# A fused attention and GLU block on one core: the orders of all five engines searched anew

## The chip, the cores and the metric

The kernel runs on one core of a Trainium2 chip. The metric is the device time of one execution in microseconds (us). A profile's span is about 2 us shorter than the device time of the same run, so spans are compared with spans only.

## The reference

All data are bfloat16: 2048 tokens (16 tiles of 128), width 448, hidden width 1792.

```python
def _A_ref(x, wqkv, wo):                 # linear attention, 16 heads of 28
    q, k, v = split_heads(x @ wqkv)
    phi = lambda t: where(t > 0, t + 1, exp(t)) + 1e-6
    pq, pk = phi(q), phi(k)
    kv = einsum("bhsd,bhse->bhde", pk, v)
    den = einsum("bhqd,bhd->bhq", pq, pk.sum(tokens)) + 1e-6
    return (einsum("bhqd,bhde->bhqe", pq, kv) / den) @ wo
def _B_ref(x, w_gate, w_up, w_down):
    return (gelu(x @ w_gate) * (x @ w_up)) @ w_down
h  = x + _A_ref(layernorm(x), wqkv, wo)
h2 = h + _B_ref(layernorm(h), w_gate, w_up, w_down)
```

The keys need all tokens before any query can be finished, so the program has a joint: everything up to `kv`, then the queries, the second layernorm, gate/up and down.

## The kernel before

Every piece of work is a task with a number. A task knows what it reads and writes; from that the program derives its semaphore waits. Which task an engine issues next is not derived: it is read from five strings of numbers, one for each of TensorE (PE), ACT, VectorE (DVE), GpSimd (POOL) and the sync engine (SP), which issues the transfers.

```python
ORDERS = (
    "26 34 32 43 41 63 66 71 76 50 ...",   # pe
    "3 25 29 30 38 39 33 42 65 47 ...",    # act
    "27 28 36 37 31 40 35 44 45 54 ...",   # dve
    "17 15 13 0 18 14 20 16 1 21 ...",     # pool
    "2 4 5 6 7 8 9 10 11 12 98 ...",       # sp
)
...
    def place(self, orders):
        self.order = {e: [self.all[int(i)] for i in o.split()] for e, o in zip(ENGS, orders)}
...
    def emit(self, ename, eng):          # cut: each task waits for what it depends on
        for t in self.order[ename]:
            ...
            ins = t.fn(eng, W) if t.mw else t.fn(eng)
```

The tasks, by the names they have in the code, sizes left out (`out2_2` is `out_2` here; the gate/up units keep theirs); the last number is the tile, the pair of tiles p, or the unit v:

- Head: `tr0_t`, `tr1_t` (transposes of tiles 0 to 3 on TensorE), `evxA_t`/`evxD_t` (their evictions), `xT_t` (the same transpose as a transfer, tiles 4 on), `k_t`, `q_t` (projections, source line L404), `ek_t`, `eq_t` (exponentials), `rq_t` (relu), `pt_t` (product of keys with the normalised input, L423), `kv`.
- Middle: `w2_g` (kv folded into wo), `dr_t`, `rd_t`, `pn_t` (denominator, reciprocal, normalised query), `tro_t` (its transpose on TensorE for tiles 0 and 1, L504), `oT_p` (as a transfer for the others), `out_t` (output projection, L523), `trh_t` and `hT_t` (the same two ways for the second layernorm), `wrap_t` (a copy that `hT_t` waits for).
- Back: `gu2_v`, `gu4_v` (gate/up units of two or four tiles), `ge_v` (gelu), `hm_v` (product of gelu and up, L625), `dwd` (load of the down weight), `down_t` (L575), `do_t` (store).

A gate/up unit contracts 448 rows as seven pieces of 64, gate in the upper 64 rows of the array and up in the lower 64, side by side:

```python
for k in range(NK):                       # NK = 7
    W(2 * (NK * jj + k))                  # first one: gate bank psG free
    e.matmul(psG[...], wgu_sb[A_, k, ...], hnT[A_, ka_, ...], start=(k == 0), stop=(k == NK - 1))   # L603
    W(2 * (NK * jj + k) + 1)              # first one: up bank psU free
    e.matmul(psU[...], wgu_sb[B_, k, ...], hnT[B_, kb_, ...], start=(k == 0), stop=(k == NK - 1))   # L605
```

There are two gate banks and two up banks, so unit v waits for the products of unit v-2. All other matmuls named here use one group of 112 or 128 rows: going from one kind to the other is a "switch of row mode".

## Time and profile before

| kernel before | median us | range | runs |
|---|---|---|---|
| ahead of the change | 194.24 | 194.19 to 194.25 | 3 |
| beside the changed kernel | 194.25 | 194.16 to 194.46 | 6 |

The profile on which the prediction rests fell in the slow state (clock 0.95). So that traces at one clock could be compared, the kernel before was profiled again, unchanged, as the run `before_again` (device time 194.41 us, span 192.67 us). I cut its span at four events: the start of `kv`, of the first gate/up unit, of unit gu4_14 and of unit gu4_28. Busy time by stretch in `before_again`; columns: stretch, length, then busy us and instruction count of PE, PEld, DVE, ACT, POOL, then clock, DMA share, GB/s:

```profile
0.00:38.23 38.23, 36.67 (x217) 20.98 (x218) 32.16 (x92) 23.86 (x70) 17.96 (x44) 1.00 0.74 179
38.23:50.79 12.56, 12.34 (x93) 7.09 (x91) 12.31 (x34) 12.09 (x32) 3.35 (x3) 1.00 0.79 137
50.79:83.39 32.60, 32.58 (x446) 23.96 (x447) 31.52 (x88) 12.53 (x37) 18.30 (x24) 1.00 0.59 122
83.39:126.10 42.71, 42.71 (x309) 20.07 (x304) 28.73 (x76) 10.69 (x34) 11.33 (x22) 1.00 0.38 70
126.10:192.67 66.57, 64.12 (x519) 35.25 (x518) 26.96 (x67) 18.44 (x56) 0.00 (x0) 1.00 0.07 22
```

Its chain that ended last, the run of work that decided when the program ended, as shares of the span by engine:

```profile
PE 88%; ACT 4%; DVE 4%; DMA 2%; POOL 1%; issue 0%; DVEq 0%; ACTq 0%; POOLq 0%
```

TensorE is busy nearly all of each stretch. In the second, VectorE and ACT are as full as TensorE; in the third, VectorE is. These two are where an order on those engines can produce a wait; in the last nobody but TensorE counts. "Busy" hides the waits of interest: a matmul that is 0.1 or 0.2 us late leaves the engine "busy" in this count. They are found only by taking each start against the start before it.

### The profile page before, as it was taken

The numbers are of one execution on the slowest core, as the hardware profiler recorded it, in microseconds if no ns is written. First come the engines' busy times: TensorE is split into PE (matmuls) and PEld (weight loads), VectorE is DVE, ScalarE is ACT, GpSimd is POOL, SyncE is SP. The second block draws the span as 40 slices with busy tenths as digits, with TensorE's granted clock in tenths as the row PEclk, the third lists the DMA queues.
The fourth block names the chain that finished last, engine by engine and source line by source line (L and its number), as shares of the span: only waits on it lengthen the run. The fifth ranks groups of instructions, "written<-read, shape, count | busy, mean of one in ns | idle before, by whom it ended". The sixth has DMA issues, their size and how long they took to land.

```text
span 197.8 us, 4145 instructions
## 1 busy us (share of the span) xinstructions
PE 193.7 (98%) x1572; PEld 106.9 (54%) x1572; DVE 132.0 (67%) x355; ACT 78.1 (39%) x226; POOL 50.7 (26%) x92
## 2 busy tenths in 40 slices
PE   7999999999999999999999999999999999999995
PEld 7554555555767776654454445444444454444454
DVE  3899988999999989988786537244445422444412
ACT  3797645599943324141330420023444200334200
POOL 7067710640451955235222024000000000000000
PEclk9999999999999999999999999999999999999999
DMA  6966449994587046420217272600200010100011
GB/s 194 375 174 88 94 96 209 221 215 63 102 291 124 16 50 117 102 53 23 56 26 153 57 56 52 133 21 30 46 0 3 0 46 4 46 0 3 0 46 46
DMA packets 35331, 16.97 MB, mean 86 GB/s; under 512 B 27696, under 2 KB 34032, under 8 KB 35312
## 3 DMA queue, kind: packets, MB, share of 16 engines
q1 hardware_dynamic: 35168, 16.60, 38.4%
q8 instruction: 12, 0.20, 0.4%
q10 hardware_dynamic: 144, 0.11, 0.2%
q14 instruction: 7, 0.06, 0.1%
HBM read 8.26 MB, written 1.84 MB: 51 GB/s over the span
## 4 chain that ended last, share of the span: by engine, by line
PE 90%; DMA 4%; DVE 4%; POOL 1%; issue 0%; DVEq 0%; POOLq 0%
PE ps L603 42%; PE ps L575 22%; PE ps L404 9%; PE ps L523 7%; PE ps L423 5%; PE ps L605 3%; DMA x_sb<-in_A_x_dram 2%; DVE st L348 2%; DMA xnT<-xnn 2%; DVE pk L417 1%; PE ps L471 0%; PE ps L462 0%; POOL wqk_sb L302 0%; PE ps L550 0%; DVE xnn L370 0%; DVE mv L349 0%
## 5 line engine op out<-in xcount | busy, mean ns | idle before, releaser
L605 PE MATMUL ps<-hnT,wgu_sb 64*128 64x512 bf16 (+1 forms) x490 | 89.9, 342 | 0.0
L603 PE MATMUL ps<-hnT,wgu_sb 64*128 64x512 bf16 (+1 forms) x490 | 89.6, 342 | 0.0
L623 ACT ACTIVATE gl<-ps 128x256 bf16<-128x256 f32 x112 | 37.1, 381 | 88.5 <-PE ps L605 86.4
L603 PEld LDWEIGHTS ps<-hnT,wgu_sb 64*128 64x128 bf16 x490 | 46.3, 96 | 35.1 <-issue 3.1
L625 DVE TENSOR_TENSOR hh<-ps,gl 128x256 bf16<-128x256 f32 x112 | 42.5, 416 | 34.0 <-ACT gl L623 33.7
L605 PEld LDWEIGHTS ps<-hnT,wgu_sb 64*128 64x128 bf16 x490 | 45.2, 96 | 3.7 <-DVE hh L625 0.5
L575 PE MATMUL ps<-wd_sb,hh 128*128 128x448 bf16 (+1 forms) x238 | 45.2, 351 | 0.0
L575 PEld LDWEIGHTS ps<-wd_sb,hh 128*128 128x128 bf16 x238 | 23.3, 99 | 21.1 <-issue 1.3
L404 PE MATMUL ps<-wqk_sb,xnT 128*128 128x448 bf16 x128 | 28.2, 362 | 0.1
L488 POOL TENSOR_TENSOR t<-pq,zbc 128x448 f32<-128x448 bf16 x15 | 16.6, 1115 | 33.3 <-DVE pq L484 20.5
L579 DVE TENSOR_TENSOR x_sb<-ps,x_sb 128x448 bf16<-128x448 f32 (+1 forms) x17 | 10.0, 592 | 19.6 <-PE ps L575 19.6
L348 DVE BATCH_NORM_STATS2 st<-x_sb 128x6 f32<-128x448 bf16 x32 | 19.1, 612 | 3.5 <-DMA x_sb<-in_A_x_dram 3.4
L404 PEld LDWEIGHTS ps<-wqk_sb,xnT 128*128 128x128 bf16 x128 | 12.3, 99 | 12.1 <-DMA xnT<-xnn 0.5
L423 PE MATMUL ps<-pk,xnn 128*128 128x448 bf16 x64 | 14.4, 363 | 0.0
L523 PE MATMUL ps<-w,pqnT 112*128 112x448 bf16 x64 | 14.1, 362 | 0.0
L558 POOL TENSOR_SCALAR hn<-x_sb,nm,rs 128x448 bf16<-128x448 bf16 x14 | 10.9, 779 | 8.1 <-DMA hnT<-hn 7.4
L529 DVE TENSOR_TENSOR x_sb<-ps,x_sb 128x448 bf16<-128x448 f32 x16 | 9.5, 617 | 3.8 <-PE ps L523 3.8
L415 ACT ACTIVATE e<-ps 128x448 bf16<-128x448 f32 x16 | 8.7, 541 | 5.4 <-PE ps L404 3.6
L417 DVE SCALAR_TENSOR_TENSOR pk<-ps,e 128x448 bf16<-128x448 f32 x16 | 9.9, 616 | 0.2
L388 POOL TENSOR_SCALAR xnn<-x_sb,nm,rs 128x448 bf16<-128x448 bf16 x12 | 9.0, 749 | 3.5 <-ACT rs L357 3.5
L423 PEld LDWEIGHTS ps<-pk,xnn 128*128 128x128 bf16 x64 | 6.5, 101 | 6.2
L495 DVE TENSOR_TENSOR pqn<-pq,rd 128x448 bf16<-128x448 bf16 x16 | 9.6, 622 | 0.0
(65 smaller groups left out, 125.0 us busy)
## 6 DMA issues: line engine op xcount, KB each, us to landing
out_dram<-x_sb SPq DMA_DIRECT2D x15, 112.0 KB, 1.7
wd_sb<-in_B_w_down_dram SPq DMA_DIRECT2D x1, 1568.0 KB, 7.7
x_sb<-in_A_x_dram SPq DMA_DIRECT2D x3, 448.0 KB, 5.4
wgu_sb<-in_B_w_gate_dram SPq DMA_DIRECT2D x1, 896.0 KB, 11.9
wgu_sb<-in_B_w_up_dram SPq DMA_DIRECT2D x1, 896.0 KB, 16.5
wqk_sb<-in_A_wqkv_dram SPq DMA_DIRECT2D x1, 672.0 KB, 4.8
wgu_sb<-in_B_w_gate_dram SPq DMA_DIRECT2D x1, 672.0 KB, 6.0
wgu_sb<-in_B_w_up_dram SPq DMA_DIRECT2D x1, 672.0 KB, 8.4
```

Source lines behind the costliest of these rows:

```text
L348: op("dve", lambda e: e.bn_stats(st[:, t, :], src_ap), [b_src], [b_st[t]], "bnst%s_%d" % (tag, t))
L404: ins = e.matmul(ps[:, bk, 0:D], xnT[:, t, k, :], wqk_sb[:, k, c0:c0 + D], start=(k == 0), stop=(k == 3))
L417: op("dve", lambda e: e.scalar_tensor_tensor(pk[:, ip, :], psK, EPS, e1[:, i, :], ALU.max, ALU.add), [b_ps[bk], b_e1[i]], [b_pk[ip]], "pk_ ...
L423: ins = e.matmul(ps[:, BK_PT[c], 0:D], xnn[:, t % XN_R, c * 128:(c + 1) * 128], pk[:, ip, :], start=(t == 0), stop=(t == T - 1))
L488: op(eng, lambda e, t=t, n=n: e.tensor_tensor(t1[:, n, :], pq[:, t, :], zbc[:, :], ALU.mult), [b_pq[t]] + b_z, [b_t1[n]], "t1%s_%d" % (eng ...
L523: ins = e.matmul(ps[:, BK_OUT[n], 0:D], pqnT[0:GW, i2, n, g, :], w2[:, g, :], start=(g == 0), stop=(g == NG - 1))
L558: op("pool", lambda e, t=t, sh=sh: e.tensor_scalar(hn[:, sh, 0:D], x_sb[:, t, :], nm2[:, t:t + 1], rs2[:, t:t + 1], ALU.add, ALU.mult), [b ...
L575: ins = e.matmul(psO, hh[:, j, (t % HR) * 128:(t % HR + 1) * 128], wd_sb[:, j, c0:c1], start=(j == 0), stop=(j == NJ - 1))
L603: e.matmul(psG[:, jj * N:(jj + 1) * N], wgu_sb[A_, k, j * 128:(j + 1) * 128], hnT[A_, ka_, c0:c0 + N], start=(k == 0), stop=(k == NK - 1))
L605: ins = e.matmul(psU[:, jj * N:(jj + 1) * N], wgu_sb[B_, k, j * 128:(j + 1) * 128], hnT[B_, kb_, c0:c0 + N], start=(k == 0), stop=(k == NK ...
L623: G.add("act", lambda e, gi=gi, cs_=cs_, psG=psG: e.activation(gl[:, gi, cs_], psG[:, cs_], AF.Gelu_apprx_tanh), r=[b_ps[BK_G[i]]], w=[b_g ...
L625: op("dve", lambda e, dst=dst, srcU=srcU, srcL=srcL: e.tensor_tensor(dst, srcU, srcL, ALU.mult), [b_ps[BK_U[i]], b_glh], [b_ar[j_][t % HR] ...
```

## The change

Tasks, transfers, buffers and sizes stay. The five strings come from a new search for a good order, in which the task times were jittered (so that an order that lives on a lucky margin scores badly) and a switch of row mode cost more than before. The diff, cut:

```diff
 ORDERS = (
-    "26 34 32 43 41 63 66 71 76 50 52 61 59 79 84 70 87 116 75 99 83 111 91 126 103 138 150 115 130 162 174 142 187"
...
+    "26 32 34 43 63 41 66 71 76 52 59 50 61 79 84 70 87 75 99 83 116 111 91 126 103 138 115 150 162 130 174 142 154"
...                                       (act, dve and pool: new orders as well)
-    "2 4 5 6 7 8 9 10 11 12 98 110 125 137 149 161 173 186 199 212 228 244 281 282 283 284 354 386 355 417 368 371"
...
+    "2 4 5 6 7 8 9 10 11 12 98 110 125 137 149 161 173 186 199 212 228 244 281 282 283 284 354 386 417 368 371 355"
...
 )
```

The same in names, TensorE's head, TensorE between kv and gate/up, the blocks of gate/up units, and SP:

```diff
-PE  tr1_0 tr0_0 tr1_1 tr0_1 q_0 k_0 k_1 q_1 tr0_2 tr1_2 tr1_3 tr0_3 k_2 q_2 pt_0 k_3 q_3 pt_1 k_4 pt_2 k_5 pt_3 k_6
+PE  tr0_0 tr1_0 tr1_1 q_0 tr0_1 k_0 k_1 q_1 tr1_2 tr0_3 tr0_2 tr1_3 k_2 q_2 pt_0 k_3 pt_1 k_4 pt_2 q_3 k_5 pt_3 k_6
...
-PE  kv q_8 w2_1 w2_2 w2_0 w2_3 q_10 tro_0 q_11 tro_1 out_0 q_9 out_1 q_12 q_15 q_14 q_13 trh_0 trh_1 out_2 gu2_0
+PE  kv q_8 w2_1 w2_3 w2_0 q_9 tro_0 w2_2 q_11 out_0 tro_1 q_10 out_1 q_12 q_15 q_14 out_2 trh_0 trh_1 q_13 gu2_0
...
-gate/up blocks: 0-1 | 2-5 | 6-7 | 8-11 | 12-16 | 17-21 | 22-27 | 28-44 | 45-55
+gate/up blocks: 0-1 | 2-5 | 6-9 | 10-11 | 12-16 | 17-27 | 28-47 | 48-55
...
-SP  oT_1 oT_2 dwd oT_3 hT_2 hT_3 hT_5 hT_4 oT_4
+SP  oT_1 oT_2 oT_3 hT_2 hT_3 dwd oT_4 hT_5 hT_4
```

## The prediction

> **What bounds the kernel now.** I read the page's first two parts, then the chain that ended last in order of time, then the busy time by stretch, and last the single TensorE rows, each start against the next start. The profiled execution has a span of 197.8 us and is marked slow (199.48 us against 194.24 us in the three timed runs), so every microsecond below is a slow-state one, at a granted clock of 0.95.
>
> ```profile
> PE 193.7 (98%) x1572; PEld 106.9 (54%) x1572; DVE 132.0 (67%) x355; ACT 78.1 (39%) x226; POOL 50.7 (26%) x92
> PE 7999999999999999999999999999999999999995
> PEclk9999999999999999999999999999999999999999
> PE 90%; DMA 4%; DVE 4%; POOL 1%; issue 0%; DVEq 0%; POOLq 0%
> ```
>
> TensorE is full from 5.4 us to the end, and 90% of the chain that ended last is TensorE itself. Busy is not peak, though, so I checked the starts. Over the whole trace matmuls follow each other at one fixed step per shape: 0.197 us for 448 columns, 0.2245 us for a pair of 64-row matmuls (gate and up together) of 512. The starts that come later than that step are few, and I added all of them: about 3.4 us. This is everything that an order of instructions can win after the head, under 2% of the time.
>
> The chain shows what they are:
>
> ```profile
> 14.40 3.85 DMA xnT<-xnn
> 18.30 0.96 PE ps L404 x4
> ...
> 117.78 11.02 PE ps L575 x56
> 128.80 0.32 PE ps L603
> 129.34 0.22 PE ps L603
> ```
>
> The first matmul of L603 after the down projection (L575) carries 0.32 us where its successors carry 0.22: it is the change from a 128-row group to two 64-row groups. Such changes occur 18 times, 9 into and 9 out of the gate/up groups, and the late start is 0.091 to 0.105 us in each: 18 x 0.095 = 1.7 us. The first two lines are another kind: the projection of tile 6 starts at 18.30, when the transpose by DMA of that tile has landed (18.25), 0.22 us late. The others: 0.48 and 0.27 us in the head (waiting for the normalised tiles 1 and 3), 0.10 and 0.04 around the small kv and w2 products, 0.16 after the first transpose of pqn (waiting for an ACT eviction that ends at 42.41), and inside three gate/up units 0.07, 0.09 and 0.19.
>
> Which engine makes those is in the busy time by stretch (columns PE, PEld, DVE, ACT, POOL, then clock, DMA share, GB/s):
>
> ```profile
> 51.40:60.00 8.60, 8.60 (x131) 6.65 (x132) 8.25 (x23) 5.18 (x14) 5.51 (x8) 0.95 0.90 243
> 60.00:70.00 10.00, 10.00 (x128) 7.05 (x123) 10.00 (x29) 3.59 (x12) 5.64 (x9) 0.95 0.33 54
> 128.70:184.10 55.40, 55.40 (x449) 26.37 (x448) 23.51 (x60) 17.77 (x54) 0.00 (x0) 0.95 0.06 18
> ```
>
> From 51 to 70 us VectorE is as full as TensorE: there its order decides which wait ends last. From 128.7 on it is under half busy and nothing but TensorE counts. In that part each gate/up unit finds its PSUM bank freed only 0.11 us ahead, but it repeats unit after unit without a late start.
>
> **What the Trainium skill says.** "TensorEngine Tiling (Array Packing)", Key Properties: "Changing tiling mode (not just tile) drains the TensorE". The trace agrees, and gives the size, about 0.095 us each way. "TensorE: Matmul & The Clock Gate", Back-to-back issue gap: N/2.4 + 2.5 ns, so 215.8 ns for 512 columns; the trace has 224.5 ns, which is 512/(2.4 x 0.95), so the step here follows the granted clock; the same page's statement that the throttle is 4/8 or 8/8 (or 13/16) does not cover the 0.95 recorded here. "DMA: Bandwidth & Descriptors", Queues, rings and completion order: on each DMA engine descriptors are consumed in ring order. Transfers issued from SP therefore stand behind one another, which is why a moved issue of the large weight matters; the trace does not contradict it.
>
> **The change, part by part.** Tasks, transfers, sizes and buffers stay; only the five orders differ. TensorE's sum of matmul steps is unchanged, so 190 us less 3.4 us of late starts cannot move.
>
> 1. Row-group changes. I counted the blocks of gate/up units in both orders. Before: units 0-1, 2-5, 6-7, 8-11, 12-16, 17-21, 22-27, 28-44, 45-55: nine blocks. After: 0-1, 2-5, 6-9, 10-11, 12-16, 17-27, 28-47, 48-55: eight. Two changes fewer x 0.095 = **-0.19 us**. This is the whole direct worth of the "dearer switches".
>
> 2. Head, to the projection of tile 6. The first two tiles are bound by the x transfers and the chain statistics, normalise, transpose, which keep their order, so the 0.48 us stays (a later small transpose moves behind the first projection, at no gain). For tiles 2 and 3 VectorE does one 0.54 us statistics less ahead of normalising tile 3 (it ended at 9.90, now about 9.5), so the 0.27 us wait goes. But the transpose whose result ACT evicts for tile 2 moves from first to third of four, and on ACT that eviction now stands behind both exponentials of tiles 0 and 1. Counting ACT's rows (relu 0.42, exponentials 0.54 and 0.54, a logarithm 0.28, from about 8.7) it ends near 10.5 in place of 10.15; the projection k2 starts near 10.55 in place of 10.21: +0.35. Against that the 0.22 us wait for tile 6's DMA transpose is swallowed. Net **+0.1 us**.
>
> 3. The projection of tile 9 now comes one 0.79 us slot earlier relative to the work ahead of it: about 22.3, and its transpose landed at 22.57 in this trace. SP issues transposes 1.3 us or more apart and that chain hardly moves. A wait of up to 0.3 us may come: **+0.1 us**.
>
> 4. kv to the first gate/up. Evictions of q7 are put ahead of q6's and q9 stands between w2 and the transpose of pqn, so the 0.16 us wait goes: **-0.16 us**.
>
> 5. Gate/up units. The hh products of unit 3 are no longer behind an added cq and aq; their last one ends about 0.35 us earlier, so the 0.07 goes; the pairs dr_12 with a batch-statistics (0.53 each) no longer stand ahead of unit 14's products (0.09), and the sequence dr_15, bnag, rd_14 (0.79 us) between unit 17 and 18 is cut up (0.19). New ones: rd_14 with pn_14 (0.70) ahead of unit 21's products, where VectorE's own gap between units is about 0.67. Net **-0.25 us**.
>
> 6. The down weight wd (1568 KB). Before, it is issued at 51.54 and lands 7.7 us later (59.24), while the first down projection starts at 67.77: 8 us of room. After, its issue stands behind oT_3, hT_2 and hT_3. hT_3 waits for wrap_3, which ended at 61.80 and moves by -0.37 (sum of VectorE durations ahead of it, in both orders); a transpose holds SP's issue about 1.3 us; so wd is issued near 62.8 and lands near 70.5 with the measured 7.7. The first down projection is now after four gate/up units: 64.5 + 4 x 1.58 + 0.1 = 70.9. Room: 0.4 us, by an estimate from durations that scatter by as much. I put **+0.15 us**: nothing in most cases, half a microsecond or more in some.
>
> Sum: -0.19 + 0.1 + 0.1 - 0.16 - 0.25 + 0.15 = -0.25 us. From 194.24: **194.0 us**. Tail: the last three stores change order, after the last add 0.4 us and a store of 1.5 us remain: 0.
>
> **Rivals.**
> (a) The orders really are better under scatter: the head is not later, tile 9 does not wait, wd is in time; then only -0.19 - 0.27 - 0.22 - 0.16 - 0.35 = -1.2 us, so 193.0. For it: the search was made for tolerance, and one order leaves longer uninterrupted gate/up blocks. Against it: half of the late starts are row-group changes, of which 16 stay. Even taking away all late starts but the 16 changes and the head's first 0.48 would give 194.24 - (3.4 - 1.5 - 0.5) = 192.8, still within 2%.
> (b) wd becomes the wait that ends last: TensorE idles at the first down projection until it lands. If wd were 1 us slower for the transposes beside it, or wrap_3 1 us later on the full VectorE, the stall is 0.6 to 1.2 us: 195.0. For it: 0.4 us of room in place of 8; against it: wd no longer shares the DMA engines with oT_2, and DMA is idle for two thirds of that stretch (share 0.33).
> (c) VectorE becomes the bound between 51 and 84 us: with the down projections moved back, units 6 to 9 run as one block, which needs 4 x 4 products and their fill work in 6.3 us. Against it: by the sum of durations the order reaches unit 6's products 1.5 to 2.2 us of work earlier than before. If wrong, +0.5: 194.7.
>
> **Range and chances.** TensorE's unmovable work fixes the lower end: 193.1 is rival (a) nearly whole. The upper end 195.2 is rival (b) with a little of (c). Beyond 2% faster (190.4) is impossible with the sum of late starts at 3.4 us and 16 changes kept; 2% slower (198.1) needs a stall of 4 us, such as wd landing that late or a die in a slower clock. So 0.01, 0.97, 0.02.
>
> **What would show it right or wrong.** Right: 16 late first matmuls of about 0.1 us at row-group changes, TensorE still at 98%, matmul steps unchanged at equal clock. Step 2: k2 at 10.5 and the chain passing through an ACT eviction there. Step 3: the chain passing through a DMA of xnT near 22 us. Step 6: the landing of wd against the start of the first L575 row; a TensorE wait on that DMA makes it rival (b). Late starts inside gate/up units around 64 to 84 us would be rival (c). A different granted clock in the timed runs would move both kernels and is no effect of the orders. The prediction fails if the late starts come to over 5 us or under 2.

## The result, and the profile after

| | median us | range | runs |
|---|---|---|---|
| before | 194.25 | 194.16 to 194.46 | 6 |
| after | 194.12 | 193.63 to 194.67 | 6 |

The ratio is 0.9994, with an interval from 0.9977 to 1.0011: the same. Ratios here are the mean time of one kernel's fast runs over that of the other's of the same rounds, so not quite the ratio of the quoted medians. The predicted 194.0 lies 0.12 us from the measured median. The changed kernel's six runs spread over 1.0 us and those of the kernel before over 0.3, but in later rounds the kernel before spread over 1.0 to 1.6 us as well, so this is not a property of the new order.

In the changed kernel's chain that ended last, the share of transfers has grown from 2% to 6%; the load of the down weight, which was not in the old chain, has 4%:

```profile
PE 84%; DMA 6%; DVE 4%; ACT 3%; POOL 1%; issue 0%; SPq 0%; DVEq 0%; POOLq 0%
```

Its busy time by stretch, cut at the same four events (columns as before):

```profile
0.00:38.23 38.23, 36.47 (x217) 20.71 (x218) 32.19 (x92) 24.25 (x70) 17.66 (x44) 1.00 0.75 180
38.23:50.95 12.72, 12.46 (x93) 6.92 (x92) 12.14 (x32) 12.16 (x32) 4.07 (x4) 1.00 0.75 132
50.95:83.55 32.60, 32.39 (x445) 24.11 (x446) 30.31 (x88) 12.28 (x36) 16.22 (x23) 1.00 0.53 121
83.55:125.63 42.08, 42.08 (x308) 21.50 (x303) 29.37 (x75) 10.97 (x34) 10.09 (x17) 1.00 0.26 53
125.63:192.20 66.57, 64.12 (x519) 35.49 (x518) 27.67 (x71) 18.44 (x56) 2.52 (x5) 1.00 0.13 34
```

Line by line against `before_again`: 0.00, +0.16, 0.00, -0.63 and 0.00, together -0.47 us of span. Three of the five stretches are equal to the last digit, but only the last because the two orders cost the same in it. The first and the third hide pairs of opposite effects. I take them in the order of the program.

**Head.** TensorE's timeline (start, length, operation, count; in brackets the idle time and what ended it) of the kernel before, in `before_again`:

```profile
10.47 1.69 PE L404 MATMUL ps<-wqk_sb,xnT 128*128 128x448 bf16 x8
...
18.54 0.93 PE L404 MATMUL ps<-wqk_sb,xnT 128*128 128x448 bf16 x4 [0.33 <-DMA xnT<-xnn]
```

and of the changed kernel:

```profile
10.79 1.69 PE L404 MATMUL ps<-wqk_sb,xnT 128*128 128x448 bf16 x8 [0.52 <-ACT xnT L383]
...
18.54 0.93 PE L404 MATMUL ps<-wqk_sb,xnT 128*128 128x448 bf16 x4
```

The first line of each is `k_2`: after the change it starts 0.32 us later, and the bracket names ACT's eviction of tile 2. The second is `k_6`: the same 18.54 in both. In the kernel before, TensorE was there early and waited for the transposing transfer `xT_6`, which landed at 18.50; after the change it arrives later and waits less. In these two traces the late eviction costs nothing. In 11 of the 13 full-clock traces `kv` starts 19.67 to 19.69 us after `k_6` (19.83 and 19.89 in the other two), so the start of `k_6` decides the length of the head.

**kv to gate/up.** The end of this stretch in the kernel before (`before_again`), TensorE:

```profile
48.39 0.94 PE L550 MATMUL ps<-ident,hn 128*128 128x128 bf16 x14
49.17 1.68 PE L523 MATMUL ps<-w,pqnT 112*128 112x448 bf16 x8
50.78 0.28 PE L603 MATMUL ps<-hnT,wgu_sb 64*128 64x256 bf16 x1
```

and in the changed kernel:

```profile
47.77 1.67 PE L523 MATMUL ps<-w,pqnT 112*128 112x448 bf16 x8 [0.26 <-DVE mv L349]
49.28 0.95 PE L550 MATMUL ps<-ident,hn 128*128 128x128 bf16 x14
...
50.95 0.28 PE L603 MATMUL ps<-hnT,wgu_sb 64*128 64x256 bf16 x1
```

`out_2` (L523, eight matmuls) now stands ahead of the transposes `trh_0` and `trh_1` (L550). By the step from the matmul before it, it is 0.42 us late. The bracket puts this down to a VectorE row that `out_2` does not read; what it needs is `oT_1`, issued at 43.55 and landed at 47.63. (In two other traces, shown below, the profile itself names that transfer. In all seven traces with this order `out_2` starts 0.14 us behind the landing of `oT_1`, whenever that was.) The transposes queue behind, their eviction on VectorE ends at 50.89, and the first gate/up unit (L603) can only start at 50.95. In six of the seven traces this stretch is 12.30 us, within 0.01, plus the late start of `out_2`. So by my estimate from these lengths the new order without that one wait would be 0.26 us shorter than the old one's 12.56.

**The down weight.** The changed kernel's chain that ended last, in order of time (start, length, what):

```profile
63.13 7.13 DMA wd_sb<-in_B_w_down_dram
70.30 2.82 PE ps L575 x14
```

`dwd` is issued at 63.13, lands at 70.25, and the first down projection starts at 70.30, 0.20 us after it could have. The kernel before had this load done about 8 us ahead. In the third stretch this +0.20 is balanced by unit gu2_5, whose late start, with the switch behind it, fell from 0.34 to 0.16.

**Gate/up units.** The fourth stretch has the gain. In unit 16, these are the gate (L603) and up (L605) matmuls of the kernel before (`before_again`):

```profile
86.41 0.38 PE L603 MATMUL ps<-hnT,wgu_sb 64*128 64x512 bf16 x1
86.62 0.39 PE L605 MATMUL ps<-hnT,wgu_sb 64*128 64x512 bf16 x1
```

and the same unit after the change:

```profile
86.57 0.38 PE L603 MATMUL ps<-hnT,wgu_sb 64*128 64x512 bf16 x1
86.59 0.38 PE L605 MATMUL ps<-hnT,wgu_sb 64*128 64x512 bf16 x1
```

Normally gate and up start at most 0.02 us apart. Before, the first up matmul came 0.21 us after its gate, because its bank was still being read. VectorE says by whom; the kernel before (`before_again`):

```profile
85.29 0.62 DVE L348 BATCH_NORM_STATS2 st<-x_sb 128x6 f32<-128x448 bf16 x1
85.82 0.74 DVE L625 TENSOR_TENSOR hh<-ps,gl 128x256 bf16<-128x256 f32 x2
```

and after:

```profile
85.69 0.75 DVE L625 TENSOR_TENSOR hh<-ps,gl 128x256 bf16<-128x256 f32 x2 [0.38 <-ACT gl L623]
```

Before, the products of unit 14 (L625, two instructions) stood behind a batch statistic; they ended at 86.56 and the up matmul followed at 86.62. After, VectorE waits 0.38 us for the gelu and is done by 86.44, ahead of need.

The lag is not paid in the unit. Gate and up run in different rows of the array and each keeps its own step (0.2158 us), so the up half stays 0.21 behind through the whole block, and the block's end is 0.21 later: it is paid once, at the next switch of row mode. The lag did not grow beyond about one step: in gu4_20 of `before_again` the first up matmul was 0.25 us late, the second gate matmul was then late as well, and the lag fell to 0.21; in gu2_5, with steps of 0.109 us, 0.25 fell to 0.11. Adding all starts that come more than 0.015 us later than their step gives about 5.0 us in `before_again` and 4.6 in the changed kernel. Of these, the switches are 18 starts in the first and 16 in the second, 0.096 us each where nothing else is late, and the matmul behind each is another 0.01 late.

### The profile page after: what moved, and what is told of

It is laid out like the page before. It is cut to its first block, busy times and chain, and to the rows that moved or that the text cites. A ratio compares the mean times of both kernels' runs of the same rounds, so it can differ in the third digit from the quotient of the medians.

```text
span 192.2 us, 4152 instructions
## 1 busy us (share of the span) xinstructions
PE 187.5 (98%) x1572; PEld 108.7 (57%) x1572; DVE 131.7 (69%) x355; ACT 78.1 (41%) x226; POOL 50.6 (26%) x92
## 4 chain that ended last, share of the span: by engine, by line
PE 84%; DMA 6%; DVE 4%; ACT 3%; POOL 1%; issue 0%; SPq 0%; DVEq 0%; POOLq 0%
PE ps L603 34%; PE ps L575 22%; PE ps L404 10%; PE ps L423 6%; PE ps L523 5%; PE ps L605 5%; DMA wd_sb<-in_B_w_down_dram 4%; DMA x_sb<-in_A_x_dram 2%; DVE hh L625 1%; DVE st L348 1%; ACT eq L431 1%; ACT pq L432 1%; DVE x_sb L529 1%; PE ps L471 0%; ACT e L415 0%
## 5 line engine op out<-in xcount | busy, mean ns | idle before, releaser
L605 PE MATMUL ps<-hnT,wgu_sb 64*128 64x512 bf16 (+1 forms) x490 | 86.6, 334 | 0.0
L603 PE MATMUL ps<-hnT,wgu_sb 64*128 64x512 bf16 (+1 forms) x490 | 86.4, 333 | 0.1
L625 DVE TENSOR_TENSOR hh<-ps,gl 128x256 bf16<-128x256 f32 x112 | 42.9, 418 | 30.9 <-ACT gl L623 30.7
L603 PEld LDWEIGHTS ps<-hnT,wgu_sb 64*128 64x128 bf16 x490 | 45.3, 94 | 28.0 <-issue 2.6
L605 PEld LDWEIGHTS ps<-hnT,wgu_sb 64*128 64x128 bf16 x490 | 42.7, 94 | 4.8 <-DVE hh L625 2.0
L575 PE MATMUL ps<-wd_sb,hh 128*128 128x448 bf16 (+1 forms) x238 | 43.6, 342 | 0.1
L575 PEld LDWEIGHTS ps<-wd_sb,hh 128*128 128x128 bf16 x238 | 23.0, 98 | 20.1 <-issue 0.8
L404 PE MATMUL ps<-wqk_sb,xnT 128*128 128x448 bf16 x128 | 27.6, 352 | 0.5 <-ACT xnT L383 0.5
L523 PE MATMUL ps<-w,pqnT 112*128 112x448 bf16 x64 | 13.6, 353 | 0.3 <-DVE mv L349 0.3
L352 POOL TENSOR_SCALAR nm<-mv 128x1 f32<-128x1 f32 (+1 forms) x19 | 4.1, 220 | 25.1 <-DVE mv L349 24.5
L523 PEld LDWEIGHTS ps<-w,pqnT 112*128 112x128 bf16 x64 | 5.6, 97 | 7.2 <-issue 1.3
## 6 DMA issues: line engine op xcount, KB each, us to landing
wgu_sb<-in_B_w_up_dram SPq DMA_DIRECT2D x1, 896.0 KB, 16.4
```

The costliest lines, as they stand in the source:

```text
L404: ins = e.matmul(ps[:, bk, 0:D], xnT[:, t, k, :], wqk_sb[:, k, c0:c0 + D], start=(k == 0), stop=(k == 3))
L523: ins = e.matmul(ps[:, BK_OUT[n], 0:D], pqnT[0:GW, i2, n, g, :], w2[:, g, :], start=(g == 0), stop=(g == NG - 1))
L575: ins = e.matmul(psO, hh[:, j, (t % HR) * 128:(t % HR + 1) * 128], wd_sb[:, j, c0:c1], start=(j == 0), stop=(j == NJ - 1))
L603: e.matmul(psG[:, jj * N:(jj + 1) * N], wgu_sb[A_, k, j * 128:(j + 1) * 128], hnT[A_, ka_, c0:c0 + N], start=(k == 0), stop=(k == NK - 1))
L605: ins = e.matmul(psU[:, jj * N:(jj + 1) * N], wgu_sb[B_, k, j * 128:(j + 1) * 128], hnT[B_, kb_, c0:c0 + N], start=(k == 0), stop=(k == NK ...
L625: op("dve", lambda e, dst=dst, srcU=srcU, srcL=srcL: e.tensor_tensor(dst, srcU, srcL, ALU.mult), [b_ps[BK_U[i]], b_glh], [b_ar[j_][t % HR] ...
```

## The experiments

Twelve kernels ran, five rounds each, all at a clock of 0.999 or 1.00, on two chips. `before_again`, `head_before`, `head_after` and `wd_early` share one set of runs of the kernel before; `fetch_shift`, `evict_tile2`, `more_switches` and `before_eq7` another, on a chip whose times scatter more (kernel before: 193.97 to 195.53); the last four a third.

My theory after the result: the change gains in the gate/up units and in two switches, and gives part back behind `oT_1` and `dwd`; the head is decided by `xT_6`. The rivals: the head costs something, through ACT's eviction of tile 2; the wait ahead of the output projection is ACT's alone and could be won; the slow transfers are due to the fetches of TensorE's own instructions.

| run | median us | ratio to before [95%] |
|---|---|---|
| before_again | 194.27 | 0.9997 [0.9981, 1.0013] |
| head_before | 194.08 | 0.9980 [0.9960, 1.0000] |
| head_after | 194.87 | 1.0024 [1.0003, 1.0044] |
| wd_early | 194.03 | 0.9984 [0.9963, 1.0005] |
| fetch_shift | 194.84 | 1.0004 [0.9971, 1.0038] |
| evict_tile2 | 195.52 | 1.0037 [1.0009, 1.0065] |
| more_switches | 195.05 | 1.0034 [0.9996, 1.0073] |
| before_eq7 | 194.43 | 0.9989 [0.9961, 1.0016] |
| after_again | 193.32 | 0.9952 [0.9927, 0.9976] |
| mid_before | 194.24 | 0.9984 [0.9961, 1.0007] |
| mid_wd | 193.34 | 0.9946 [0.9926, 0.9967] |
| mid_wd_merge | 193.78 | 0.9968 [0.9947, 0.9989] |

### before_again: the kernel before, unchanged

```diff
 (no edit)
```

> The kernel before, unchanged, to get its profile at the full clock (the one at hand has 0.95) and to see what a comparison of a kernel with itself reads. Ratio 1.000 within 0.002. Theory A (late starts only: row-group changes, edges of transfers): gate/up units of four tiles step at 1.511 us as in the kernel after, 18 row-group changes at 0.088 us, the projection of tile 6 still waits for its DMA transpose, and all late starts together come to 4 to 4.8 us. Rival B (at the full clock the release of PSUM banks is too late, as only 0.11 us stood there at 0.95): units over 1.53 us each and late starts inside most of them.

Measured: 194.27 us, ratio 0.9997. It gives the full-clock trace used above. At a clock of 0.95 three waits inside gate/up units were 0.07, 0.09 and 0.19 us; at full clock the corresponding ones are 0.26, 0.21 and 0.26. TensorE's step for 448 columns is 0.189 us in place of 0.197, while the mean VectorE and ACT instruction takes 0.43 and 0.41 us in both traces, so a margin that just held at 0.95 no longer does. The slow-state trace had understated what the orders can win: all late starts come to about 5.0 us (expected 4 to 4.8) in place of 3.4. Rival B did not come; the units of four tiles still step at 1.511 us.

### head_before and head_after: one half of each kernel

```diff
 head_before: all engines
-    <after's order up to q_6 (PE), rq_5 (ACT), aq_5 (DVE), normP_15 (POOL), dwu1 (SP)>
+    <before's order up to there, then after's>
 head_after: the mirror image
-    <before's order up to there>
+    <after's order up to there, then before's>
```

> Orders of before up to q6 (PE), rq5 (ACT), aq5 (DVE), normP15 (POOL), dwu1 (SP), orders of after behind that. Theory A (what the tile-2 projection loses in the new head is covered by the wait for the tile-6 transpose, so the heads are equal): same as the kernel after within 0.25 us, 193.9 to 194.3. Rival C (the new head costs its visible 0.68 us wait in full): 193.5, about 0.5 us under the kernel after.

> The mirror image: orders of after up to the same cut, orders of before behind it. Theory A: same as before within 0.25 us, 194.0 to 194.4. Rival C: about 194.7, 0.5 us over the kernel before.

Measured: 194.08 and 194.87 us. In the traces `kv` starts at 37.90 in `head_before` and 38.03 in `head_after`. The gain in the stretch from gu4_14 to gu4_28 goes with the back half: 42.05 in `head_before`, 42.99 in `head_after`. Over the traces of all runs except `evict_tile2`, `kv` starts at 38.11 on average with before's head (six traces, 37.78 to 38.55) and 38.20 with after's (six, 37.94 to 38.54): no difference can be seen. One cost is visible, but small: with after's head TensorE comes to `k_6` 0.05 to 0.13 us after `xT_6` has let it in three of these six traces (`after_again`, `wd_early`, `more_switches`), with before's head in none. The gain behind gu4_14, on the other hand, is in every trace: 42.05 to 42.09 us in all ten with after's order there, 42.70 to 42.99 in the three with before's. So the timed -0.2% of `head_before` fits the back half. The time of `head_after`, 194.87, is where rival C had put it (194.7), and Theory A missed it (194.0 to 194.4); but its trace does not show the loss in the head. It is 0.49 us longer than that of `before_again`, but its head is 0.20 shorter: the excess lies in the three stretches behind `kv` (12.75, 32.81 and 42.99 us against 12.56, 32.60 and 42.71), though their orders are those of before. By single starts it is 0.19 us ahead of the w2 products, 0.21 at gu2_7 (waiting for `hT_3`) and 0.26 in units gu4_25 to gu4_27. Whether another head leaves ACT and VectorE worse placed for them, or this is scatter, stays open.

### wd_early: the down weight at its old place

```diff
-SP  oT_1 oT_2 oT_3 hT_2 hT_3 dwd oT_4
+SP  oT_1 oT_2 dwd oT_3 hT_2 hT_3 oT_4
```

> The kernel after with one move: the down weight is issued behind oT_2, as in the kernel before, and no longer behind hT_3. Theory A: it lands about 60, the first down projection no longer waits (0.20 us in the profile), 193.8 to 194.0, and the runs scatter less than the 1.04 us of the kernel after. Rival D (the weight's traffic then slows oT_3, hT_2 and hT_3, and the wait for hT_3 grows by as much): no gain, 194.1 or more, with the late start before the second gate/up unit of tiles 2 and 3 over 0.35 us in place of 0.23.

Measured: 194.03 us, ratio 0.9984. The two stretches from kv in `wd_early` (columns as before):

```profile
38.54:51.59 13.05, 12.47 (x92) 6.93 (x92) 12.15 (x32) 12.15 (x32) 4.39 (x4) 1.00 0.79 133
51.59:83.91 32.32, 32.32 (x446) 24.11 (x447) 30.34 (x88) 12.28 (x36) 15.88 (x22) 1.00 0.53 121
```

The stretch with the down weight's wait falls from 32.60 to 32.32: the wait of 0.20 us is gone. The other 0.10 is unit gu2_7, which waits 0.14 us for `hT_3` in place of 0.24, the opposite of rival D. The runs scatter over 1.2 us, not less as I had expected. The stretch ahead of it, untouched by this edit (the old place is behind `oT_2`), is 13.05 in place of 12.72 because `oT_1` landed later there; here the profile names that transfer as the wait, 0.6 us. So one trace shows both parts, and why a single time can't separate them.

### fetch_shift: is it the instruction fetch that slows the transposes?

The trace shows 16 KB packets on a DMA queue of kind "instruction", twelve in an execution; the one at about 15.2 to 16.4 us runs beside `xT_6`. That they bring TensorE's instructions is my inference. I moved TensorE's instruction count by replacing the warm-up matmuls with fewer, wider ones.

```diff
-    WARM = 40                         # matmuls of 128 columns
+    WARM, WN = 22, 232                # matmuls of 232 columns, fewer instructions
-    ones_bf = sb("ones_bf", [128, 128], BF16)
+    ones_bf = sb("ones_bf", [128, 232], BF16)
```

> The kernel after with its 40 warming matmuls of 128 columns replaced by 22 of 232 columns: the same time on TensorE, 36 instructions fewer ahead of everything else, so each later 16 KB fetch of TensorE's instructions comes 18 matmuls later. Theory E (a DMA transpose in flight when such a fetch comes takes 1.0 to 1.7 us longer): the fetch at 15.35 moves to about 18.8, the tile-6 transpose takes 2.5 us in place of 4.2 and lands near 16.8, the tile-8 one is the slow one instead; oT_1 takes 3.2 in place of 4.1 and the 0.42 us wait of the first output projection goes; hT_3 stays slow (the fetch moves by 1 us only). Ratio to before 0.997, 193.6. Rival F (the slow transposes are slow from other traffic on the DMA engines, and the fetch only happens to be near): tile 6 and oT_1 land within 0.3 us of where they did, 194.1.

Measured: 194.84 us, ratio 1.0004; no gain. The fetches moved by only 0.5 to 4 us (15.35 to 16.02 for the one beside `xT_6`, where 18.8 was expected), so `xT_6` still had one beside it and still took 4.23 us. Further back, where the fetch did move, three transposes that were fast became slow exactly where it now came: `oT_4` 3.08 to 4.07 us, `hT_15` 3.10 to 4.65, `hT_14` 2.93 to 4.26. Over 14 traces, and counting also the 8 KB and smaller packets of a second instruction queue, of 238 transposes without a fetch in flight one was over 0.5 us slower than its kind's median (2.49 us for `xT`, 3.06 for `oT`, 2.94 for `hT`); of 224 with one, 81 were, by up to 1.9 us. This is an association with one partly successful intervention behind it. For `xT_6` the fetch as cause is not shown: a 16 KB fetch was in flight in all 14 traces (3.58 to 4.23 us). For `oT_1` it is doubtful: the one slow transpose without a fetch is `oT_1` itself, 3.95 us in `mid_before`, as long as most of those with one (3.36 to 4.87). It also runs beside the gate/up weight load.

The run also confirms the wait of the middle stretch. In its timeline of TensorE, `out_2` carries the transfer's name (`pqnT<-pqn` is `oT_1`):

```profile
48.51 1.67 PE L523 MATMUL ps<-w,pqnT 112*128 112x448 bf16 x8 [1.05 <-DMA pqnT<-pqn]
```

The stretch from kv to gate/up was 13.51 us here, the longest of all.

### evict_tile2: tile 2's eviction earlier on ACT

```diff
-PE  ... tr1_2 tr0_3 tr0_2 tr1_3 ...
+PE  ... tr1_2 tr0_2 tr0_3 tr1_3 ...
-ACT ... rstd1_3 rq_0 ek_0 ek_1 ... evxA_2 ...
+ACT ... rstd1_3 evxA_2 rq_0 ek_0 ek_1 ...
```

> The kernel after with two moves: the transpose of tile 2 that ACT evicts goes first of its four, and its eviction goes ahead of the relu of tile 0 and the exponentials of tiles 0 and 1. Theory A: the projection k2 starts at about 10.2 in place of 10.79, but the projection of tile 6 starts where it did, at 18.5, as its DMA transpose decides; its late start grows from 0.17 to about 0.7; time as the kernel after, 194.1. Rival C (the 0.68 us at k2 is paid in full): k6 starts near 18.0 and the time is 193.5.

Measured: 195.52 us, ratio 1.0037. TensorE's timeline of this run:

```profile
10.61 0.55 PE L404 MATMUL ps<-wqk_sb,xnT 128*128 128x448 bf16 x2 [0.66 <-ACT pq L432]
11.99 1.46 PE L404 MATMUL ps<-wqk_sb,xnT 128*128 128x448 bf16 x6 [0.83 <-DVE xnT L385]
```

`k_2` starts only 0.18 us earlier, then its third matmul waits 0.83 us for the other half of tile 2, evicted by VectorE behind `ck_1`, which needs `ek_1`, which my edit had pushed back. The edit was built badly (the transpose that ACT evicts also went second of its four, not first as I had written) and does not test what it was meant to. It does show the size of the head's margin: `q_2` comes at 12.52, 0.97 us later than in the changed kernel, whose `k_6` still waits 0.18 us for `xT_6`; the remaining 0.79 must arrive behind it, and `k_6` (19.34, no wait) and `kv` (39.02) are both 0.8 us later. The change's own slip of 0.32 is within the 0.50 that the kernel before waited there.

### more_switches: six switches more

```diff
-PE  ... gu4_47 down_9 down_8 down_11 down_10 gu4_48 gu4_49 gu4_50 ...
+PE  ... gu4_47 down_9 gu4_48 down_8 gu4_49 down_11 gu4_50 down_10 ...
```

> The kernel after with six more row-group changes and nothing else: in the late part the four down projections of tiles 8 to 11 are no longer in one piece but alternate with gate/up units 48 to 50 (VectorE's order follows). VectorE is half idle there. Theory A: 22 late starts at changes in place of 16, 0.09 us each, +0.54 us: 194.6 to 194.8. Rival G (a change costs more than its late first matmul shows, as the drained array also delays evictions, or less because it overlaps with a wait): over +1 us, or under +0.2.

Measured: 195.05 us, ratio 1.0034. The chain that ended last, in the piece that was changed, and the last stretch of this run:

```profile
156.27 2.75 PE ps L575 x14
159.02 0.32 PE ps L603
```

```profile
125.81:193.00 67.19, 64.74 (x519) 34.05 (x518) 27.74 (x71) 18.43 (x56) 2.52 (x5) 1.00 0.13 34
```

Down projections and units alternate here, and the first gate matmul (L603) behind a down projection (L575) carries the 0.32 us of a switch in place of 0.21. The stretch is longer by 0.62 us (67.185 unrounded against 66.567), 0.10 us for each of six switches; all six late starts are 0.095 or 0.096 us. This is the direct price of a switch, with no wait mixed in, and so the worth of the two saved ones is 0.2 us.

### before_eq7: the kernel before, with one exponential put ahead on ACT

```diff
-ACT ... rq_7 ... eq_7 ...
+ACT ... rq_7 eq_7 ...
```

> The kernel before with one move: on ACT the exponential of q tile 7 goes directly behind the relu of q tile 7, three places earlier. Theory A (the 0.39 us that TensorE waits behind the first transpose of pqn comes from that eviction alone): that late start goes, and 0.2 to 0.4 us of it reach the first gate/up unit (50.79 in the kernel before at full clock): 193.8 to 194.0. Rival H (VectorE is full in this stretch, 10.6 of 10.9 us, and the wait only moves to the transposes of pqn and hn behind it): first gate/up unit not over 0.1 us earlier, 194.2.

Measured: 194.43 us, ratio 0.9989. TensorE's timeline in `before_again`, then in this run:

```profile
42.10 0.93 PE L404 MATMUL ps<-wqk_sb,xnT 128*128 128x448 bf16 x4 [0.22 <-ACT eq L431]
```

```profile
42.04 0.92 PE L404 MATMUL ps<-wqk_sb,xnT 128*128 128x448 bf16 x4
43.18 0.43 PE L504 MATMUL ps<-ident,pqn 128*112 128x128 bf16 x4 [0.22 <-DVE pqn L495]
```

The wait for ACT is gone and a wait for VectorE has come at the next transpose, `tro_1`. The stretch is 12.59 us in place of 12.56. So in the order of before, where three engines are full in this stretch, the wait that I counted as a gain in step 4 could not be won by this one move: the next one stands behind it. That does not hold for every order: the changed kernel's stretch without the wait of `out_2` is 12.30 us.

### after_again and three mixtures

```diff
 after_again: (no edit to the changed kernel)
 mid_before:  up to the first gate/up unit
-    <after's orders up to out_2 (PE), tbl2 (ACT), evhD_1 (DVE), t1p_5 (POOL), oT_2 (SP)>
+    <before's orders up to there, then after's>
 mid_wd:      as mid_before, and
-SP  oT_2 oT_3 hT_2 hT_3 dwd
+SP  oT_2 dwd oT_3 hT_2 hT_3
 mid_wd_merge: as mid_wd, and
-PE  gu4_47 down_9 down_8 down_11 down_10 gu4_48 ... gu4_55 down_12 ...
+PE  gu4_47 gu4_48 ... gu4_55 down_9 down_8 down_11 down_10 down_12 ...
```

> The kernel after, unchanged, on the chip of the next three, so that the sections can be compared in pairs. Ratio to before 0.998 to 1.000. Sections by the start of TensorE's work, as in its first profile: first gate/up unit about 12.7 us behind kv, unit 14 another 32.6 us, unit 28 another 42.1 us, end another 66.6 us.

> All five orders of before up to the first gate/up unit, those of after behind it (the down weight behind hT_3 as there). Theory A (what the change wins behind the pqn transpose it loses again at the first two-tile output projection, which stands ahead of the hn transposes and waits for oT_1): kv to first gate/up unit 12.5 to 12.6 us in place of 12.7 in the kernel after, and less scatter; the rest as in the kernel after; ratio to before 0.997, a little under the kernel after. Rival I (the new order of this stretch is neutral or better, and the loss is scatter of the landing alone): 12.7 or more, ratio as the kernel after or above.

> The same with the down weight issued behind oT_2. Theory A: no wait for it, the stretch from the first gate/up unit to unit 14 takes 32.3 us in place of 32.6; ratio to before 0.9955. Rival D (hT_3 pays for it): 32.6.

> The same again with the down projections of tiles 8 to 11 moved behind the last gate/up unit, so that units 28 to 55 run as one block: two row-group changes fewer, 14 in all. Theory A: 0.18 us less from unit 28 to the end, 66.4 in place of 66.6; ratio to before 0.9945. Rival G (a change in this part is not worth its late first matmul): same as the run before it within 0.05 us from unit 28 on, or a later end as the stores crowd at the end.

Measured: 193.32, 194.24, 193.34 and 193.78 us. The stretch from kv to gate/up in `mid_before`:

```profile
37.94:50.50 12.56, 12.34 (x92) 7.08 (x91) 12.10 (x32) 12.09 (x32) 3.48 (x4) 1.00 0.78 137
```

In `mid_wd` and `mid_wd_merge` it is 12.56 too, as in `before_again`: with before's order this stretch nearly repeats (12.59 in `before_eq7`, 12.75 in `head_after`), with after's it went from 12.51 to 13.51 over seven traces (mean 12.86), following the landing of `oT_1`. In `mid_before` the down weight was late. Its chain that ended last:

```profile
61.94 7.98 DMA wd_sb<-in_B_w_down_dram
...
69.96 2.07 PE ps L575 x10
```

The load took 7.98 us here in place of 7.13, and TensorE waited 0.41 for it (the switch and the lag of the unit ahead taken off); the third stretch is 32.72. Over the seven traces with `dwd` at its new place that wait was 0 to 0.47 us (mean 0.22, none in two of them); over the six with the old place it was 0. In `mid_wd` it is gone, but that stretch is still 32.58, because unit gu2_7 waited 0.41 us for `hT_3` (0.22 and 0.24 in the kernel before and in the changed kernel). It looks as if the old place had this price, as rival D has it, but the other traces do not bear that out: the wait for `hT_3` was 0 to 0.43 us in the six with the old place (mean 0.20; `mid_wd_merge`, with the orders of `mid_wd` up to there, had none and 32.31 us) and 0 to 0.39 in the seven with the new one (mean 0.16).

I had expected `mid_before` a little under the changed kernel; its six runs have a median 0.9 us above those of `after_again`. They fall into two groups, two at 193.6 and four from 194.2 to 194.5; the profiled one is of the first, so no trace shows what the others lost. `mid_wd` (193.34) and `after_again` (193.32) are equal. In `mid_wd_merge` two switches fewer were meant to gain 0.2 us, but my order put `down_10` and `down_12`, which use the same PSUM bank, back to back. TensorE in this run:

```profile
179.20 6.04 PE L575 MATMUL ps<-wd_sb,hh 128*128 128x448 bf16 x31 [0.72 <-DVE x_sb L579]
```

It waits for VectorE to empty that bank: 0.88 us late by the step. The last stretch is 67.25 = 66.57 - 0.20 + 0.88. This is a fault of the edit. No version clearly beats the changed kernel.

## Why the prediction was right

The time, its class and its main reason held: TensorE's fixed work cannot be moved by an order, 16 of 18 switches stay, and all late starts together are a few microseconds. The sum came out near for reasons that only partly match its terms: step 4 was off by +0.32 us and step 5 by -0.37, and that these two cancel is luck. So is the 0.12 us between the predicted and the measured median; in the second comparison the changed kernel's median was 193.32. From the two full-clock traces:

| step | predicted us | measured us |
|---|---|---|
| 1 two switches fewer | -0.19 | -0.21 |
| 2 head, eviction of tile 2 | +0.1 | 0 |
| 3 tile 9 | +0.1 | 0 |
| 4 kv to gate/up | -0.16 | +0.16 |
| 5 gate/up units | -0.25 | -0.62 |
| 6 down weight | +0.15 | +0.20 |
| sum | -0.25 | -0.47 |

- **Step 1 was right**, and `more_switches` measured its unit price separately: 0.10 us (the table has twice 0.096, with the 0.01 of the matmul behind each).
- **Step 2 had the mechanism right and the net wrong.** `k_2` did slip, behind ACT's eviction of tile 2, to 10.79 (predicted 10.55). The wait it uses up behind `xT_6` was larger at full clock, 0.50 us in place of the 0.22 of the slow-state trace, so in this pair of traces all of the slip was swallowed; in three others 0.05 to 0.13 us of it was left, about what I had put. The 0.27 us wait for the normalised tile 3 did not go either: the changed kernel has 0.22 us there, ahead of `k_2`, which waits for ACT anyway.
- **Step 3 did not happen.** `xT_9` landed at 21.72 and the projection of tile 9 started at 22.34.
- **Step 4 was wrong in sign.** I took away the wait at the transpose of pqn, and it did go (0.39 us at full clock; 0.26 of it, net, would have reached the end of the stretch). What I did not work out was what the new order puts next: `out_2` ahead of the transposes of the second layernorm, so that `oT_1` is needed at 47.35 and lands at 47.63. That is a margin of less than zero on a transfer that scatters by up to a microsecond. `before_eq7` showed for the old order that removing this wait alone only hands it on.
- **Step 5 was right in sign and mis-sized, -0.62 for -0.25**: 0.42 in the fourth stretch (0.63 less the two switches) and 0.20 at unit gu2_5. The three places that I named are the ones that improved; I read their sizes from a trace at a clock of 0.95, where TensorE gave VectorE 5% more time. No run changed VectorE's order there alone: that it makes the gain is read from the traces, where the products end before the bank is needed. Rival (c), VectorE as a new bound between 51 and 84 us, did not come: that stretch has VectorE at 30.31 us busy, 1.2 less than before.
- **Step 6 was right**, even in its shape ("nothing in most cases, half a us or more in some"): issue 63.13 against 62.8, landing 70.25 against 70.5, waits of 0 to 0.47 us. In the two full-clock traces no transfer of SP landed before one that was issued ahead of it, as the prediction had assumed. Rival (b), 0.6 to 1.2 us, was not reached. `wd_early` shows the wait is due to the place of the load.
- **Rival (a)**, all going well at 193.0, is nearer than I thought: `after_again` has a median of 193.32, with `kv` at 37.94 and `out_2` only 0.12 us late (12.51 for the middle stretch).

The condition of failure that I set, late starts of over 5 us or under 2, was touched: about 5.0 for the kernel before at full clock, 4.6 after.

What stays open: the two comparisons of the same two kernels gave 0.9994 and 0.9952, with intervals that do not overlap, and the fast runs of the changed kernel went from 193.09 to 194.67. The traces of both show where such a difference can come from (the spans are 192.20 and 191.52; the parts are -0.29 up to `kv`, -0.21 behind `oT_1`, -0.19 around the down weight), but not why these transfers land earlier on one occasion. The best single statement is the mean of the two, about -0.3%. What repeats in every trace is the gain of 0.6 us behind gu4_14; what varies is what the transfers take back ahead of it. The new order leaves three transfers (`xT_6`, `oT_1`, `dwd`) with no room; in the kernel before `oT_1` and `dwd` had some. So a search under jittered times still left margins near zero.

## What to carry to other kernels

Before estimating what a new order wins, sum every start that comes later than its step, in a trace at the clock of the timed runs: that sum bounds the gain, and a slow-state trace understates the waits on engines that do not slow down. For each wait that an order removes, look for the next one behind it on a full engine, and for each transfer that it moves, set the landing against the need; a margin smaller than the transfer's scatter will be paid in some of the runs.

## What the Trainium skill lacked or had wrong

- "TensorEngine Tiling (Array Packing)", Key Properties, says that a change of tiling mode drains TensorE, without a figure. Here it is 0.096 us of late start for each change at full clock, and 0.10 us when six were added (0.62 us). The page also does not say how far one row half can fall behind the other: an up matmul that starts 0.21 us late leaves its half behind until the next change, where the 0.21 us is paid once; a lag of 0.25 us held up the gate half too and fell to one step, 0.21 us for 512 columns and 0.11 for 256.
- "DMA: Bandwidth & Descriptors" has nothing on transposing transfers beside instruction fetches. Without a fetch in flight 237 of 238 stayed within 0.5 us of their median (2.49, 3.06 or 2.94 us); with one, 81 of 224 were slower, by up to 1.9 us. One run that moved the fetches made three fast transposes slow where they now came; for the two that matter most the cause is not settled, and `oT_1` was slow once without a fetch (3.95 us).
- "TensorE: Matmul & The Clock Gate" lists throttle ratios of 4/8, 8/8 and 13/16; the first profile of the kernel before ran at 0.95. Its issue gap of N/2.4 + 2.5 ns, 215.8 ns for 512 columns, agrees with the 0.2158 us measured at full clock in each row half.
